# Attention's TensorE work in source order, with the products with V behind the next chunk's score tiles

## Chip, cores and metric

One core of a Trainium2 chip runs the whole program once. The time is device microseconds (us) of one execution, the median over the runs shown. The core's engines are named as in the profile: PE (TensorE: matmuls, with PEld for its weight loads), ACT (ScalarE), DVE (VectorE), POOL (GpSimd) and SP (which issues most DMAs).

## What is computed

Three stages follow each other: attention over 4 x 8 heads with queries pooled by two, a routed mixture of experts with a skip, and a gated feed-forward layer. The change touches the first stage alone.

```python
def _attn_ref(q, k, v):                      # (4, 8, 1152, 64) each
    B, H, S, D = q.shape
    factor = 2
    scale = 1.0 / np.sqrt(D)
    q_pool = q.reshape(B, H, S // factor, factor, D).mean(axis=3)
    scores = scale * np.matmul(q_pool, k.transpose(0, 1, 3, 2))
    scores = scores - np.max(scores, axis=-1, keepdims=True)
    attn = np.exp(scores)
    attn = attn / (np.sum(attn, axis=-1, keepdims=True) + 1e-09)
    return np.matmul(attn, v).astype(np.float32)

def reference(**kwargs):
    ...
    attn_out = _attn_ref(**attn_kwargs)
    B, H, S, D = attn_out.shape
    x = np.ascontiguousarray(attn_out.transpose(0, 2, 1, 3)).reshape(B * S, H * D)
    x = _moe_ref(x=x, **moe_kwargs)
    return _moe2_ref(x=x, **moe2_kwargs)
```

## The kernel before

`attention` works on two heads at a time: 16 pairs, p = 0 to 15, in a loop that begins at line 786. The 1152 keys of a head are cut into nine chunks of 128, c = 0 to 8. The 576 pooled queries of a head are cut into two halves of 288, n = 0 and 1.

For one chunk, `qk` (lines 665 to 676) makes four score tiles, one for each head h and half n. A tile is two matmuls into one PSUM tile `s`: the high parts (line 670) and the low parts with the subtracted maximum (line 671). ACT then writes the tile's exponential into the chunk's tile `P` (line 674). There are three PSUM tiles `s` (pool `ps_s`), so the fourth score tile from here waits until ACT has read this one.

`pv` (lines 689 to 695) multiplies `P` with V and adds up into the output tile `o`. Its matmuls have 64 columns: head 0 writes partitions 0 to 63 and head 1 partitions 64 to 127. A chunk has four such products, and `values` (lines 794 to 800) does two chunks at a time, c-2 and c-1, at c = 2, 4, 6 and 8; chunk 8 comes at c = 0 of the next pair. In each pair but the first, c = 4 also makes the row sums of the pair before (`sums`, line 699; `sum_up`, line 704, again with 64 columns). The sums over chunks themselves are added up on POOL (`rowsum`, line 678).

While pair p runs, the same engines prepare later pairs, as side work that `spread` sets between the steps of the loop:

- for pair p+1 the maxima of the scores: `m_tile` (line 630), 27 tiles `mx` that PE makes and DVE reduces (line 643), then `m_fin`;
- for pair p+2 the transposes of K (`t_k`, line 591, six of three blocks) and of Q (`t_q`, line 604, two of four blocks and two of one); ACT copies each out of PSUM, a K transpose with two copies, a Q transpose with three (lines 614 and 619);
- for pair p+3 the splitting of K and Q into high and low parts (`split_pieces`, line 576; on ACT lines 543 and 563), and the loads;
- in pairs 4, 5, 8, 9, 12 and 13 five blocks of the routing per batch (`Route.rows`, line 272), with a store `xd<-xr` each; in pairs 6 and 10 a ranking (`rank`).

Tiles of the side work share three PSUM tiles of the pool `ps_m`. In the last pair the weights of the first expert are loaded into buffers that attention has done with (`load_w`, line 444; group 3 into the sum buffer `acc` of pair 14, which `sums` at c = 4 reads last).

What sets the order: the steps are written down one after the other, but inside the loop a scheduler orders each engine's instructions by what it expects to be ready. So a product with V stands on PE wherever the scheduler saw a wait. Only the start-up (`ramp`, lines 522 to 774) and the later mixture of experts keep the order of the source.

Of the kernel before, what the change touches and what calls it, by code (L numbers as in the profile page):

```python
# [20 lines left out]
ET = mybir.EngineType  # L21


def spread(main, sides):
    ev = []
    for i, f in enumerate(main):
        ev.append((i, 0, len(ev), f))
    for j, (pieces, a, b) in enumerate(sides):
        pieces = list(pieces)
        for i, f in enumerate(pieces):  # L30
            ev.append((a + (b - a) * (i + 0.5) / len(pieces), 1 + j, len(ev), f))
    for e in sorted(ev, key=lambda e: e[:3]):
        e[3]()
# [3 lines left out]
def body(ctx, tc, q, k, v, w_skip, w_gate, w1, w2, m2_gate, m2_val, m2_out, out):  # L37
# [155 lines left out]
    NFG = 4  # L193
# [220 lines left out]
    def after_all(i, names):  # L414
        for a in names:
            tc.add_manual_dep(i.ins, a.name, mybir.DependencyInfo(mybir.DependencyClass.Sync, mybir.DependencyReason.DATA))
# [27 lines left out]
    def load_w(which, i, r, after=(), gs=range(NFG), pool=False):  # L444
        o, n = LIST[which]
        e = nc.values_load(info[0:1, o + i:o + i + 1], engines=(ET.Pool if pool else ET.SP,), min_val=0, max_val=E - 1)
        for g in gs:
            fs = slice(g * FG, (g + 1) * FG)
            src = w1[bass.ds(e, 1), :, fs] if r == "r1" else w2[bass.ds(e, 1), fs, :]
            d = (nc.gpsimd if pool else nc.sync).dma_start(raw[r, g][:], src.rearrange("o (c p) f -> p (o c) f", p=128))  # L450
            if not g:
                after_all(d, after)
# [18 lines left out]
    def attention(st):  # L471
# [193 lines left out]
        def qk(p, h, c, n):  # L665
            s = s_[p]
            cs = slice(c * 128, (c + 1) * 128)
            ns = slice(64 * h + n * 288, 64 * h + (n + 1) * 288)
            ps = ps_s.tile([128, 512], FP, tag="s", name="s")
            nc.tensor.matmul(ps[:, 0:288], s["ks"][:, h, cs], s["qsh"][:, h, ns], start=True, stop=False)  # L670
            nc.tensor.matmul(ps[:, 0:288], s["ks2"][0:69, h, cs], s["qsl"][0:69, h, ns], start=False, stop=True)  # L671
            if h == 0 and n == 0:
                s["P", c] = pp.tile([128, 2, 2, 288], FP, tag="P", name="P")
            i = nc.scalar.activation(s["P", c][:, h, n], ps[:, 0:288], AF.Exp, scale=0.5 / float(D) ** 0.5)  # L674
            if (h, c, n) == (0, 0, 0):
                mark[p] = i.ins.name
# [12 lines left out]
        def pv(p, c, n):  # L689
            s = s_[p]  # L690
            if c == 0 and n == 0:
                s["o"] = ps_o.tile([128, 2, 512], FP, tag="o", name="o")
            for h in range(2):
                nc.tensor.matmul(s["o"][h * 64:(h + 1) * 64, n, 0:288], s["vt"][:, h, c, :], s["P", c][:, h, n, :],  # L694
                                 start=c == 0, stop=c == NC - 1)
# [5 lines left out]
        def evac(p):  # L701
            nc.scalar.activation(xview(p), s_[p]["o"][:, :, 0:288], AF.Copy)

        def sum_up(p, src, first=True, last=True):
            if first:
                s_[p]["sm"] = ps_m.tile([128, 512], FP, tag="m", name="sm")
            for h in range(2):
                for n in range(2):
                    o = h * SQ + n * 288
                    nc.tensor.matmul(s_[p]["sm"][n * 64:(n + 1) * 64, 0:288], ones[:, 32 - 16 * h:96 - 16 * h], src[:, o:o + 288],  # L710
                                     start=first and not h, stop=last and h == 1)
# [7 lines left out]
        def sums(p):  # L719
            sum_up(p, s_[p]["acc"][:])  # L720
            sum_out(p)
            del s_[p]
# [58 lines left out]
        def sum_part(c):  # L781
            s = s_[last]
            src = s["acc"][:] if c == PEC - 1 else s["P", c][:].rearrange("p h n c -> p (h n c)")
            sum_up(last, src, c == PEC - 1, c == NC - 1)

        for p in range(NP):
            main = []
            for c in range(NC):
                pcs = [(p, c - 2), (p, c - 1)] if c and c % 2 == 0 else [] if c else [(p - 1, NC - 1)]
                for n in range(2):  # L790
                    if p or (c, n) not in early:
                        main.append(lambda c=c, n=n: qk(p, 0, c, n))

                def values(c=c, pcs=pcs):
                    if p and c == 4:
                        sums(p - 1)
                    for pc in pcs:
                        if pc[0] >= 0:
                            pv(*pc, 0)
                            pv(*pc, 1)  # L800
                main.append(values)
                main.append(lambda c=c: qk(p, 1, c, 0))
                if c == 0 and p:
                    main.append(lambda: evac(p - 1))

                def tail(c=c):
                    qk(p, 1, c, 1)
                    if p < last or c < PEC:
                        rowsum(p, c)
                main.append(tail)  # L810
            n = len(main)
            sides = []
            if not p:
                sides.append((split_pieces(2) + [lambda: load(3)], n * 0.6 / 9, n * 2 / 9))
            if p + 1 < NP:
                sides.append((m_pieces(p + 1), 0, n * 8.6 / 9))
            if p:
                sides.append(([lambda: m_fin(p, 1)], 1.5, 1.5))
            if p + 2 < NP:
                sides.append((t_pieces(p + 2, qs=False), n * 1.8 / 9, n * (5.2 if p else 6) / 9))  # L820
                sides.append((t_pieces(p + 2, ks=False), n * (5.2 if p else 6) / 9, n * (7 if p else 8) / 9))
            if p + 3 < NP:
                if p:
                    load(p + 3)
                sides.append((split_pieces(p + 3), n * (5.4 if p else 6.4) / 9, n * 8.6 / 9))
            if p + 1 < NP:
                load_v(p + 1)
            if p and p % HP == 0:
                routes.append(Route(p // HP - 1, routes[-1].scatters if routes else ()))
                bp = routes[-1].pieces()  # L830
            if p >= HP and p % HP < 2:
                rw = [lambda t=t, r=routes[-1]: r.rows(t) for t in range(G)]
                sides.append((rw[2:], 0, n * 4 / 9) if p % HP else (rw[:2], n * 5.2 / 9, n * 8.9 / 9))
            if p > HP and p % HP:
                cut = [0, *(CUT if p < last - 2 else CUL), len(bp)]
                sides.append((bp[cut[p % HP - 1]:cut[p % HP]], n * (4.5 if p == last - 2 else 1) / 9, n * (8.9 if p < last else 2.5) / 9))
            if 0 <= p - CP0 < 2 * len(first):
                if not (p - CP0) % 2:
                    cp = conv0.pieces(first[(p - CP0) // 2])
                    sides.append((cp[:1], n * 0.3 / 9, n * 0.3 / 9))  # L840
                    sides.append((cp[1:2], n * 6.5 / 9, n * 6.5 / 9))
                else:
                    sides.append((cp[2:], n * 3 / 9, n * 3 / 9))
            if p == last:
                sides.append(([list_a], n * 0.2 / 9, n * 0.2 / 9))
                sides.append(([lambda: load_w("A", 0, "r1", (), range(NFG - 1))], n * 1.5 / 9, n * 1.5 / 9))
                sides.append(([lambda: load_w("A", 0, "r1", (), range(NFG - 1, NFG))], n * 4.6 / 9, n * 4.6 / 9))
                sides.append(([lambda: load_ids("A", 0, routes[-1].scatters), lambda: gather("A", 0, 0)], n * 2.6 / 9, n * 3.5 / 9))
                pair = lambda i: psum[0]("xt")[:].rearrange("p (c n) -> p c n", c=2)
                sides.append(([lambda c2=c2: xt("A", 0, 0, c2, pair) for c2 in range(2)], n * XA / 9, n * 8.8 / 9))  # L850
                sides.append(([lambda g=g: split("r1", g, nc.gpsimd if g in AP1 else nc.vector) for g in range(3)], n * SA / 9, n * 8.8 / 9))
                sides.append(([lambda c=c: sum_part(c) for c in range(PEC - 1, NC - 1)], n * 8.3 / 9, n))
            spread(main, sides)
        sum_part(NC - 1)
        for n in range(2):
            pv(last, NC - 1, n)
# [331 lines left out]
    with ExitStack() as st:  # L1188
        routed = attention(st)
# [35 lines left out]
```

## Time and profile before

| what | value |
|---|---|
| runs | 1246.89, 1247.16, 1249.86 us; median 1247.16 us |
| profiled execution: time, span | 1245.98 us, 1244.4 us |
| PE busy, share of the span | 1183.8 us, 95% |
| PE weight loads busy | 968.2 us, 78% |
| DVE, ACT, POOL busy | 697.8, 631.3, 549.1 us |
| mean granted clock of TensorE | 0.984 of full speed |
| first score tile of pairs 0, 1, 2, 3, 7, 8, 15 | 25.9, 68.8, 100.6, 132.9, 276.7, 309.0, 554.3 us |

The span runs from the first to the last instruction. Busy time of PE is modelled: matmuls overlap, and a row's duration is longer than the distance to the next row's start, which is what one matmul costs in a stream. Of a timeline's row the first number is therefore the one to compare. A product with V is two rows of the trace for one matmul of the program; "x4" of line 694 is two products. The attention stage ends near 593 us; the stages behind it are not changed.

### The profile page before, as it was taken

What the parts mean: (1) busy time and instruction counts of PE and PEld (TensorE: products, weight loads), DVE (VectorE), ACT (ScalarE), POOL (GpSimd) and SP (SyncE); (2) the same over time, 40 slices, a digit from 0 to 9 for tenths busy, and PEclk for the clock granted to TensorE, in tenths of its full rate; (3) what the DMA queues carried; (4) which work ended last, traced back from release to release, by engine and by line L of the source; (5) the groups of instructions that cost most, each with busy time, mean ns of one, the idle gap of its engine ahead of it and who ended that gap; (6) DMA issues with size and microseconds to landing.
All of it is one profiled execution on the core that took longest, in us unless ns stands there. A gap on an engine that the chain in (4) does not pass through costs nothing. (4 is left out here: it accounts for less than half of the span.)

```text
span 1244.4 us, 19070 instructions
## 1 busy us (share of the span) xinstructions
PE 1183.8 (95%) x6950; PEld 968.2 (78%) x6950; DVE 697.8 (56%) x1379; ACT 631.3 (51%) x1440; POOL 549.1 (44%) x328
## 2 busy tenths in 40 slices
PE   5999999999999999998789987999999999999998
PEld 3777776667776777675678876788898999989997
DVE  5555565655656565664756584927447374443333
ACT  5777775777757786654245375635223141221111
POOL 5878886779857997572332353202001020100000
PEclk9899999999999999998999998999999999999999
DMA  6311122111222111003486683522102020000012
GB/s 187 84 58 58 58 75 92 41 59 58 83 68 75 59 56 46 15 19 86 130 274 203 205 283 107 167 71 68 34 18 86 1 78 24 18 1 1 10 68 76
DMA packets 76618, 99.48 MB, mean 80 GB/s; under 512 B 6600, under 2 KB 50760, under 8 KB 76490
## 3 DMA queue, kind: packets, MB, share of 16 engines
q1 hardware_dynamic: 73290, 91.05, 22.9%
q0 software_dynamic: 3200, 6.86, 1.7%
q8 instruction: 64, 1.05, 0.3%
q14 instruction: 64, 0.52, 0.2%
HBM read 84.71 MB, written 12.53 MB: 78 GB/s over the span
## 5 line engine op out<-in xcount | busy, mean ns | idle before, releaser
L643 DVE TENSOR_REDUCE m<-mx 128x1 f32<-128x384 f32 x432 | 228.8, 555 | 178.2 <-PE mx L641 175.0
L685 POOL TENSOR_TENSOR acc<-acc,P 128x1152 f32<-128x1152 f32 x106 | 281.7, 2658 | 79.5 <-ACT P L674 43.0
L1115 PE MATMUL g<-xh,wc 128*128 128x384 f32 x1152 | 303.9, 337 | 2.0 <-ACT xh L1103 2.0
L674 ACT ACTIVATE P<-s 128x288 f32<-128x288 f32 x576 | 212.4, 411 | 107.4 <-PE s L671 101.1
L1115 PEld LDWEIGHTS g<-xh,wc 128*128 128x128 f32 x1152 | 208.3, 188 | 8.8 <-ACT xh L1103 7.5
L694 PE MATMUL o<-P,vt 128*64 128x288 f32 x1152 | 207.7, 424 | 2.3 <-ACT P L674 2.3
L1115 PE MATMUL g<-xl,wc 128*128 128x384 f32 x576 | 194.5, 338 | 0.0
L670 PE MATMUL s<-qsh,ks 128*128 128x288 f32 x576 | 180.9, 322 | 2.0 <-ACT P L674 1.3
L641 PE MATMUL mx<-ks,qsh 128*128 128x384 f32 x480 | 169.5, 382 | 4.6 <-DVE lp L295 3.4
L147 POOL TENSOR_TENSOR wc<-ct,wc 128x512 fp32r<-128x512 f32 x30 | 41.7, 1402 | 290.9 <-ACT wc L146 227.9
L671 PE MATMUL s<-qsl,ks 69*128 69x288 f32 x576 | 169.7, 302 | 0.0
L1142 PE MATMUL o<-wc,ah 128*128 128x512 f32 x432 | 137.4, 395 | 3.2 <-ACT ah L1129 3.2
L670 PEld LDWEIGHTS s<-qsh,ks 128*128 128x128 f32 x576 | 110.4, 192 | 33.9 <-issue 22.3
L694 PEld LDWEIGHTS o<-P,vt 128*64 128x64 f32 x1152 | 84.3, 137 | 61.7 <-issue 22.8
L1126 DVE TENSOR_TENSOR sg<-sg,g 128x384 f32<-128x384 f32 x72 | 39.8, 552 | 147.1 <-PE g L1115 133.4
L641 PEld LDWEIGHTS mx<-ks,qsh 128*128 128x128 f32 x480 | 87.6, 193 | 44.4 <-issue 17.4
L671 PEld LDWEIGHTS s<-qsl,ks 69*128 69x128 f32 x576 | 110.5, 192 | 0.0
L1115 PEld LDWEIGHTS g<-xl,wc 128*128 128x128 f32 x576 | 108.4, 188 | 2.1 <-DVE xl L1104 0.3
L1124 ACT ACTIVATE sg<-g 128x384 f32<-128x384 f32 x72 | 35.1, 488 | 143.9 <-PE g L1115 143.9
L1142 PEld LDWEIGHTS o<-wc,ah 128*128 128x128 f32 x432 | 79.6, 188 | 20.3 <-ACT ah L1129 6.6
L1129 ACT ACTIVATE ah<-sg 128x384 fp32r<-128x384 f32 x72 | 37.6, 522 | 107.9 <-DVE sg L1126 107.9
L1142 PE MATMUL o<-wc,al 128*128 128x512 f32 x216 | 85.5, 396 | 0.6 <-DVE al L1130 0.5
(277 smaller groups left out, 1676.6 us busy)
## 6 DMA issues: line engine op xcount, KB each, us to landing
r<-in_moe_w_dram SPq DMA_DIRECT2D x28, 512.0 KB
vt<-in_v_dram SPq DMA_DIRECT2D x16, 576.0 KB
kt<-in_k_dram SPq DMA_DIRECT2D x15, 576.0 KB
qraw<-in_q_dram SPq DMA_DIRECT2D x32, 256.0 KB
xT<-in_moe_w_dram SPq DMA_DIRECT2D x14, 512.0 KB
r<-in_moe_w_gate_dram SPq DMA_DIRECT2D x12, 512.0 KB
r<-in_moe_w_val_dram SPq DMA_DIRECT2D x12, 512.0 KB
r<-in_moe_w_out_dram SPq DMA_DIRECT2D x12, 512.0 KB
```

What stands on the lines that cost most here:

```text
L147: eng.tensor_tensor(w[:, 1], t[:], w[:, 0].bitcast(FP), op=ALU.subtract)
L641: nc.tensor.matmul(ps[:, 0:384], s["qsh"][:, g, c * 128:(c + 1) * 128], s["ks"][:, g, js], start=i == 0, stop=i == len(pr) - 1)
L643: nc.vector.tensor_reduce(s["m3"][:, 5 * h + t, j:j + 1], ps[:, 0:384], axis=AX, op=ALU.max)
L670: nc.tensor.matmul(ps[:, 0:288], s["ks"][:, h, cs], s["qsh"][:, h, ns], start=True, stop=False)
L671: nc.tensor.matmul(ps[:, 0:288], s["ks2"][0:69, h, cs], s["qsl"][0:69, h, ns], start=False, stop=True)
L674: i = nc.scalar.activation(s["P", c][:, h, n], ps[:, 0:288], AF.Exp, scale=0.5 / float(D) ** 0.5)
L685: i = eng.tensor_tensor(a, s["P", 0][:] if c == 1 else a, s["P", c][:], op=ALU.add)
L694: nc.tensor.matmul(s["o"][h * 64:(h + 1) * 64, n, 0:288], s["vt"][:, h, c, :], s["P", c][:, h, n, :], start=c == 0, stop=c == NC - 1)
L1115: nc.tensor.matmul(ps[:], w[:, a, fs], b[:], start=n == 0, stop=n == 3 * KD - 1)
L1126: nc.vector.tensor_tensor(sg[:], sg[:], vv[:], op=ALU.mult)
L1129: nc.scalar.activation(ah[:], sg[:], AF.Copy)
L1142: nc.tensor.matmul(ps[:], a[:, us], w[:, b, :], start=n == 0, stop=n == 3 * GF - 1)
```

## The change

Inside the loop PE now keeps the order of the source; the other engines are still ordered by the scheduler. For c > 0 `values` is called behind the fourth score tile of its chunk, not between the heads. In the last pair the load of weight group 3 is placed at 5.1/9 of the steps, not 4.6/9, which is again behind `sums`.

```diff
--- before.py
+++ after.py
@@ -783,6 +783,8 @@
             src = s["acc"][:] if c == PEC - 1 else s["P", c][:].rearrange("p h n c -> p (h n c)")
             sum_up(last, src, c == PEC - 1, c == NC - 1)
 
+        steady = tc.manual_schedule(engines={ET.PE})
+        steady.__enter__()
         for p in range(NP):
             main = []
             for c in range(NC):
@@ -798,7 +800,8 @@
                         if pc[0] >= 0:
                             pv(*pc, 0)
                             pv(*pc, 1)
-                main.append(values)
+                if not c:
+                    main.append(values)
                 main.append(lambda c=c: qk(p, 1, c, 0))
                 if c == 0 and p:
                     main.append(lambda: evac(p - 1))
@@ -808,6 +811,8 @@
                     if p < last or c < PEC:
                         rowsum(p, c)
                 main.append(tail)
+                if c:
+                    main.append(values)
             n = len(main)
             sides = []
...
-                sides.append(([lambda: load_w("A", 0, "r1", (), range(NFG - 1, NFG))], n * 4.6 / 9, n * 4.6 / 9))
+                sides.append(([lambda: load_w("A", 0, "r1", (), range(NFG - 1, NFG))], n * 5.1 / 9, n * 5.1 / 9))
...
             spread(main, sides)
+        steady.__exit__(None, None, None)
         sum_part(NC - 1)
```

PE in pair 1, in the second half of chunk 6. In a row's names `s` is a score tile, `tq` a Q transpose, `mx` a maximum tile, `o<-P` a product with V; the numbers tell tiles apart. Before:

```order
L694 MATMUL o_928<-P_1002,vt_493 64x288 x3
L641 MATMUL mx_1103<-ks_2_112,qsh_2_118 128x384
L670 MATMUL s_1106<-qsh_1_117,ks_1_111 128x288
L671 MATMUL s_1106<-qsl_1_120,ks2_1_114 128x288
L608 MATMUL tq_1110<-idr_65,qhl_770 128x128 x4
L694 MATMUL o_928<-P_1002,vt_493 64x288
L694 MATMUL o_928<-P_1058,vt_493 64x288
L641 MATMUL mx_1118<-ks_2_112,qsh_2_118 128x384
L694 MATMUL o_928<-P_1058,vt_493 64x288 x3
L670 MATMUL s_1132<-qsh_1_117,ks_1_111 128x288
L671 MATMUL s_1132<-qsl_1_120,ks2_1_114 128x288
```

The same place with the change:

```order
L608 MATMUL tq_1112<-idr_65,qhl_776 128x128 x4
L641 MATMUL mx_1120<-ks_2_112,qsh_2_118 128x384
L670 MATMUL s_1123<-qsh_1_117,ks_1_111 128x288
L671 MATMUL s_1123<-qsl_1_120,ks2_1_114 128x288
L670 MATMUL s_1130<-qsh_1_117,ks_1_111 128x288
L671 MATMUL s_1130<-qsl_1_120,ks2_1_114 128x288
L641 MATMUL mx_1135<-ks_2_112,qsh_2_118 128x384
L608 MATMUL tq_1138<-idr_65,qhl_776 128x128
L694 MATMUL o_948<-P_1004,vt_495 64x288 x4
L694 MATMUL o_948<-P_1060,vt_495 64x288 x4
L641 MATMUL mx_1151<-ks_2_112,qsh_2_118 128x384
```

The eight products of chunks 4 and 5 stood as 3, 2 and 3 between single steps; now they stand together, behind all of chunk 6.

ACT at the same place, around the last Q transposes (`qsh`, `qsl`: copies of a transpose; `P<-s`: an exponential; `qhl`: the split of Q). Before:

```order
L674 ACTIVATE P_1101<-s_1106 128x288
L614 ACTIVATE qsh_0_116<-tq_1110 64x512 x2
L619 ACTIVATE qsl_0_119<-tq_1110 64x512
L674 ACTIVATE P_1101<-s_1132 128x288
L614 ACTIVATE qsh_0_116<-tq_1139 64x128 x2
L619 ACTIVATE qsl_0_119<-tq_1139 64x128
L674 ACTIVATE P_1101<-s_1144 128x288
L674 ACTIVATE P_1155<-s_1152 128x288
L674 ACTIVATE P_1155<-s_1157 128x288
L563 ACTIVATE qhl_1130<-qp_1129 128x10x64
```

With the change:

```order
L674 ACTIVATE P_1103<-s_1108 128x288
L614 ACTIVATE qsh_0_116<-tq_1112 64x512 x2
L619 ACTIVATE qsl_0_119<-tq_1112 64x512
L674 ACTIVATE P_1103<-s_1123 128x288
L674 ACTIVATE P_1103<-s_1130 128x288
L614 ACTIVATE qsh_0_116<-tq_1138 64x128 x2
L619 ACTIVATE qsl_0_119<-tq_1138 64x128
L563 ACTIVATE qhl_1128<-qp_1127 128x10x64
L674 ACTIVATE P_1157<-s_1154 128x288
```

ACT has the same work here; three exponentials changed sides of a copy.

## Rows read from the trace of the kernel before

**Rows 1.** The page: PE's total, and its row of DVE's reductions.
```profile
PE 1183.8 (95%) x6950; PEld 968.2 (78%) x6950; DVE 697.8 (56%) x1379; ACT 631.3 (51%) x1440; POOL 549.1 (44%) x328
...
L643 DVE TENSOR_REDUCE m<-mx 128x1 f32<-128x384 f32 x432 | 228.8, 555 | 178.2 <-PE mx L641 175.0
```

**Rows 2.** Busy time by stretch, pair 2: length, PE, PEld, DVE, ACT, POOL, clock, DMA.
```profile
100.60:132.90 32.30, 32.30 (x214) 24.36 (x213) 17.23 (x33) 24.24 (x64) 26.94 (x13) 1.00 0.18 56
```

**Rows 3.** Timeline of PE, pairs 7 and 8: start, duration, line, what, count.
```profile
303.65 0.71 PE L694 MATMUL o<-P,vt 128*64 128x288 f32 x4
...
305.71 0.34 PE L641 MATMUL mx<-ks,qsh 128*128 128x384 f32 x1
305.98 0.70 PE L694 MATMUL o<-P,vt 128*64 128x288 f32 x2
306.61 0.40 PE L670 MATMUL s<-qsh,ks 128*128 128x288 f32 x1
306.85 0.30 PE L671 MATMUL s<-qsl,ks 69*128 69x288 f32 x1
...
314.92 2.16 PE L694 MATMUL o<-P,vt 128*64 128x288 f32 x16
```

**Rows 4.** Timeline of ACT, pair 7, behind the products at c = 4.
```profile
293.75 0.86 ACT L674 ACTIVATE P<-s 128x288 f32<-128x288 f32 x2 [2.91 <-PE s L671]
294.51 0.48 ACT L598 ACTIVATE ks<-tk 128x384 fp32r<-128x384 f32 x1
...
295.25 0.70 ACT L674 ACTIVATE P<-s 128x288 f32<-128x288 f32 x2
295.83 1.20 ACT L614 ACTIVATE qsh<-tq 64x512 fp32r<-64x512 f32 x2
...
297.67 0.41 ACT L674 ACTIVATE P<-s 128x288 f32<-128x288 f32 x1
297.97 1.16 ACT L543 ACTIVATE khl<-kt 128x1152 fp32r<-128x1152 f32 x1
299.03 0.40 ACT L674 ACTIVATE P<-s 128x288 f32<-128x288 f32 x1
299.32 0.54 ACT L614 ACTIVATE qsh<-tq 64x128 fp32r<-64x128 f32 x2
...
300.17 0.71 ACT L674 ACTIVATE P<-s 128x288 f32<-128x288 f32 x2
...
305.00 0.75 ACT L563 ACTIVATE qhl<-qp 128x640 fp32r<-128x640 f32 x1
```

**Rows 5.** Timeline of PE, pair 7, the same place.
```profile
293.42 0.30 PE L671 MATMUL s<-qsl,ks 69*128 69x288 f32 x1
293.55 0.34 PE L641 MATMUL mx<-ks,qsh 128*128 128x384 f32 x1
293.73 0.29 PE L670 MATMUL s<-qsh,ks 128*128 128x288 f32 x1
...
294.00 0.38 PE L595 MATMUL tk<-idr,khl 128*128 128x128 f32 x3
294.22 0.37 PE L670 MATMUL s<-qsh,ks 128*128 128x288 f32 x1
```

**Rows 6.** Timeline of PE and of DVE, pair 5: a routing block and its store.
```profile
203.45 1.24 PE L286 MATMUL xr<-iw,xT 128*128 128x146 f32 x8
204.43 0.43 PE L641 MATMUL mx<-ks,qsh 128*128 128x384 f32 x1
...
206.92 0.56 DVE L292 TENSOR_TENSOR xr<-xr,rs 128x384 f32<-128x384 f32 x1 [1.46 <-DMA xd<-xr]
```

**Rows 7.** Busy time by stretch, and PE's timeline, in pair 0 behind the start-up.
```profile
34.00:38.00 4.00, 2.80 (x17) 1.96 (x15) 2.45 (x8) 3.89 (x9) 3.68 (x7) 0.88 0.57 102
38.00:42.00 4.00, 3.31 (x12) 2.81 (x12) 2.54 (x5) 3.40 (x9) 0.00 (x0) 0.50 0.59 169
...
39.55 0.61 PE L670 MATMUL s<-qsh,ks 128*128 128x288 f32 x1 [0.69 <-ACT qsl L619]
```

## The prediction

> **What bounds the kernel now.** I read the page first: PE is busy 95% of the span, DVE 56% [rows 1]. Then the stretches of busy time, one for each pair, cut at the first score tile. In pair 2, as in 3, 7 and 11 ("plain" pairs, without routing), PE is busy for 32.30 of 32.30 us; POOL, the next, for 26.94, ACT for 24.24 [rows 2]. So PE bounds the stage on average, and a gain has to be work that PE need not do, or does more cheaply.
>
> The Trainium skill (its page "Trainium Kernel Development and Optimization", section "Performance Expectations") calls matmul busy time a bad metric, since matmuls are pipelined, and weight-load busy time a good one. Weight loads are busy for 24.36 of the 32.30 us; by that rule up to 7.9 us of a pair might be had, by the busy row nothing.
>
> The timeline of PE shows what could be cheaper [rows 3]. Products with V cost by the slot of two, one for each head: two last 0.71 us, eight 2.16, so a slot is (2.16 - 0.71)/3 = 0.483. A lone product lasts 0.70, as long as two. So an odd burst (a row of products between other steps) pays half a slot for nothing. And each burst pays at its ends. Start to start, the burst before the score tile at 306.61 takes 0.63 us, 0.15 above its slot. The maximum tile ahead of it takes 0.27 where another takes 0.18 (293.55 to 293.73 [rows 5]): 0.09. The score matmul behind it takes 0.24 where another takes 0.13 (293.42 to 293.55 [rows 5]): 0.11. Together 0.35 us for a burst, however long.
>
> **What the change brings on PE.** In the order of PE's instructions I counted bursts of lines 694 and 710: 179 before, 80 now; 92 were odd, none is now. 99 x 0.35 = 34.7 us, and 92/2 = 46 slots x 0.483 = 22.2: together **56.9 us less work on PE**. In the last pair, 4 bursts and 5 odd ones of these (4 x 0.35 + 2.5 x 0.483 = 2.6) count for nothing: its end waits for weights whose loads come no earlier.
>
> **What it takes away.** A scattered product is also what PE does while it waits. In the second half of a pair ACT is the slower one. ACT's timeline behind the products of c = 4, pair 7 [rows 4], gives the prices, start to start: the two copies of a K transpose 0.74, of two exponentials 0.58 to 0.72, the three copies of a Q transpose of 512 columns 1.84, of 128 columns 0.85, the split of K 1.06, that of Q 0.75. ACT is hardly ever idle there, and so before the change PE filled up with products. With source order PE reaches the eight products of c = 6 too late and those of c = 8 last, and stands at a score tile until an exponential has freed `s`. ACT's order with the change, from the end of the c = 4 burst: K copies 0.74, two exponentials 0.6, Q copies 1.84, two 0.6, K split 1.06, Q copies 0.85, two 0.6, Q copies 1.84, two 0.6, Q copies 0.85, Q split 0.75: 10.3 us until only exponentials at 0.30 are left. It begins some 0.5 us in, with the first score tile, so the exponential of chunk 7's second tile ends at 11.1. That tile's buffer then takes the first score tile of chunk 8; three more at the pace of ACT and PE, and the burst of c = 8 begins near 12.9. By itself PE would be there at 9.5: 16 score tiles at 0.27 (the two starts 0.13 or 0.14 [rows 5]) are 4.3, a K transpose 0.22 ([rows 5]: 294.00 to 294.22), ten blocks of Q at a third of that 0.7, ten maxima at 0.18 and a small transpose 2.0, together 7.2; the burst of c = 6 adds 2.3 (four slots and 0.35). So **3.4 us are lost in each of the 14 pairs that prepare Q for p+2: 47.6**. Before, from 293.2 to 309.0, this stretch took 15.8 us with eight products more; the working gives 12.9 + 2.3 = 15.2 after, so a plain pair gains little there. Bounds for the loss: 2.5 if ACT starts with tiles left over and copies less late, 4.3 if the first exponential comes 0.9 later; I take the middle, since the durations are rows of the same place. That is +-12.6 over 14 pairs.
>
> Some work hides in this wait. In pairs 4, 8 and 12 two routing blocks are PE's there, eight matmuls of which take 203.45 to 204.43, 0.98 [rows 6]; I take 1.75 of the two. For the 12 narrow matmuls of a ranking in pairs 6 and 10 I take 0.6, between 0 and 12 at the 0.13 of a score matmul, 1.6. 3 x 1.75 + 2 x 0.6 = **6.4 back**. For small waits elsewhere (a maximum tile that DVE is late with, where a product no longer steps in) I allow 0.2 in 13 pairs: **2.6**; bounds 0, and 0.85 each (a rival below).
>
> **Edits that cost nothing.** V's later place issues no DMA and no work for another engine. The `P` tiles are read a chunk's step later; POOL and ACT had spare time for that [rows 2]. On POOL the split and sum of Q move one row sum ahead; POOL has 32.30 - 26.94 = 5.4 us a pair idle. On SP the load of V stands one place later, and in pairs 5 and 9 the first routing store is behind three more loads of Q. That makes what waits for the store late, which is DVE (below), and behind it PE's tile; the loads behind it come a pair ahead of their use. The weight group at 5.1/9 comes (0.5/9) x 34 = 1.9 us later and is used after attention, which then still has some 15 us to run: nothing, and 1.9 at most if that cover is gone.
>
> **Sum.** -56.9 + 2.6 + 47.6 - 6.4 + 2.6 = -10.5. Against the profiled execution's own 1245.98 that is 1235.5; the median of the runs is 1.2 above it, so **1237 us**.
>
> **Rivals.**
>
> *The clock falls (slower).* In pair 0, where ACT copies transposes and PE waits for it, the granted clock went from 0.88 to 0.50 of full speed, 1.2 GHz, with PE busy for 2.80 of 4 us and a wait of 0.69 [rows 7]. The change makes such a stretch in 14 pairs, PE waiting for ACT a third of the time. Then the burst of c = 6 takes 4.6 for 2.3, and the ACT-bound wait can't hide it: 14 x 2.3 = 32, 1269 us; in half of the pairs 1253. From 5 pairs on it uses up the gain. Against it: the score tiles between waits go on, and PE has some 70% of the stretch's time in work, more than in that row.
> The Trainium skill ("TensorE: Matmul & The Clock Gate", "Why this matters for your kernels") asks only for no long idle gaps between bursts; by that rule waits of some tenths of a microsecond leave the clock alone, and this rival has no chance. The trace differs: the clock is at 0.50 around a wait of only 0.69 [rows 7]. Chance 0.22.
>
> *Three tiles in `ps_m` (same).* DVE takes 0.555 for a maximum [rows 1]; ten of them lie between the bursts of c = 2 and c = 4: 5.55 against PE's own 4.7 there (eight score tiles 2.2, ten maxima 1.8, three K transposes 0.7). If PE waits for DVE in order, 0.85 x 13 = 11 is lost: 1248. For it: DVE's idle time ahead of these ended nearly always with PE [rows 1], so now DVE is ahead; against, three buffers smooth that. Chance 0.16.
>
> *The routing's stores are hidden (faster).* In pair 5, DVE waits 1.46 us for the store `xd<-xr` [rows 6], twice a pair in six pairs: 17.5 us. If it lies beside the new wait for ACT, it no longer counts: 1219. Against: in pairs 5, 9 and 13 the blocks stand ahead of c = 4, outside that stretch. Chance 0.10.
>
> *The change doesn't bring what it says.* If the 0.35 is not the price of a switch but a wait for the score tile or for P, a burst fewer brings nothing, and only 22.2 of slots is gained: about 1270. Against: the same excess stands at bursts of every length. Chance 0.05.
>
> **How the numbers follow.** 0.47 is left for my forecast of 1237, whose own bounds give 1224 to 1250. The range, 1217 to 1266, adds the same-case, most of the routing's stores and most of the clock's; it leaves out the dearest part of the clock (0.07), the price rival (0.05) and tails of the first (0.06). A measurement tells 0.3%, 3.7 us, from no change: faster is 0.40 of my forecast's, 0.10 of the stores' and 0.05 of the others'; same 0.05 of mine, 0.10 of the maxima's and 0.03 of the clock's; slower 0.19 of the clock's, the price's 0.05 and tails of 0.03.
>
> **What would show it.** Right: 80 bursts, mostly of 2.1 us start to start; plain pairs of 31 to 33 us; PE waits some 45 us in all for ACT's `P` ahead of line 670, between chunks 5 and 8 of pairs 0 to 13; granted clock at 1.00 there; pairs 4 to 6 shorter by two microseconds or more than before. Wrong: the wait at line 670 below 25 or above 65 us; a clock below 0.95 in the pairs; idle time of PE that DVE's `m` ends; bursts whose neighbours still take 0.27 and 0.24.

## The result and the profile after

The change takes 1261.51 us (median of 4 runs, 1259.25 to 1264.03) against 1247.3 before: 1.0121 of before, interval 1.0098 to 1.0145. It is slower, by 14 us where the forecast had 10 less. (Each ratio in this text is against the kernel before as measured beside that run, with medians of 1247.3 to 1250.4, so equal times can have unequal ratios.)

The page of the profile after (for the rows of before, [rows 1]):

```profile
PE 1166.0 (93%) x6950; PEld 977.5 (78%) x6950; DVE 696.0 (55%) x1379; ACT 630.9 (50%) x1440; POOL 550.3 (44%) x328
...
L643 DVE TENSOR_REDUCE m<-mx 128x1 f32<-128x384 f32 x432 | 230.4, 555 | 204.6 <-PE mx L641 197.8
...
L670 PE MATMUL s<-qsh,ks 128*128 128x288 f32 x576 | 181.6, 321 | 16.1 <-ACT P L674 14.2
```

PE is busy for 17.8 us less than before, and the span is 13.2 us longer (1257.6 against 1244.4). So PE does cost less, and stands still more.

Where in the program? The stretches of busy time are cut here at the small transpose of maxima half a chunk into each pair (line 654), in both traces alike; the first number is the length, the last but two the granted clock. Before, all of pairs 1 to 13, then pairs 2, 3, 4 and 15:

```profile
68.12:526.26 458.14, 454.72 (x2926) 330.22 (x2925) 271.15 (x618) 326.86 (x846) 357.29 (x166) 1.00 0.19 60
101.27:133.56 32.29, 32.29 (x214) 24.35 (x213) 17.23 (x34) 24.23 (x64) 26.93 (x13) 1.00 0.18 56
133.56:165.81 32.25, 32.25 (x214) 24.26 (x213) 19.00 (x39) 25.09 (x66) 26.86 (x13) 1.00 0.19 56
165.81:201.49 35.68, 35.68 (x235) 26.13 (x233) 21.62 (x51) 25.39 (x66) 28.67 (x13) 1.00 0.23 73
...
554.96:592.00 37.04, 33.71 (x199) 20.83 (x198) 18.52 (x30) 17.13 (x42) 13.96 (x9) 0.91 0.26 72
```

After, all of pairs 1 to 13, then pairs 1, 2, 3, 4 and 15:

```profile
73.16:545.75 472.59, 439.64 (x2920) 335.98 (x2919) 273.67 (x618) 325.35 (x843) 354.51 (x164) 0.95 0.19 58
73.16:106.24 33.08, 30.99 (x215) 23.58 (x213) 17.37 (x34) 24.25 (x64) 24.26 (x12) 1.00 0.18 55
106.24:140.17 33.93, 32.09 (x214) 24.38 (x213) 17.27 (x34) 24.31 (x64) 27.84 (x13) 0.95 0.19 55
140.17:176.26 36.09, 33.61 (x214) 24.95 (x213) 19.31 (x39) 25.16 (x66) 29.12 (x14) 0.91 0.22 64
176.26:210.85 34.59, 32.89 (x234) 26.02 (x233) 21.89 (x51) 25.03 (x66) 25.61 (x12) 1.00 0.20 65
...
572.88:607.80 34.92, 29.85 (x199) 20.14 (x198) 17.55 (x30) 17.07 (x42) 11.50 (x9) 0.90 0.27 77
```

Attention ends 15.8 us later (607.8 against 592.0): pair 0 takes 5.0 more (to 73.16 against 68.12), pairs 1 to 13 take 14.5 more (472.59 - 458.14), pairs 14 and 15 together 3.7 less. (The cut puts some 1.3 us on pair 0 that pairs 1 to 13 lose: before, pair 1's transpose stands at 68.12, ahead of the pair's first score tile at 68.8, while in pair 2 it stands behind it, at 101.27 against 100.6. So pair 1 after is compared with pair 2 before, which does the same work.) Behind attention 2.6 come back; why was not followed up. The clock tells the pairs apart. Pair 4, with two routing blocks behind c = 4 and a clock of 1.00, is 1.1 faster than before. Pair 3, at 0.91, is 3.8 slower.

One place makes it. Pair 2 in steps of 2 us, from the end of the c = 4 burst to the c = 6 burst:

```profile
124.00:126.00 2.00, 1.68 (x14) 1.43 (x13) 1.11 (x2) 1.99 (x5) 0.00 (x0) 1.00 0.00 0
126.00:128.00 2.00, 1.66 (x11) 1.18 (x10) 1.37 (x2) 1.97 (x4) 0.52 (x1) 1.00 0.00 0
128.00:130.00 2.00, 0.85 (x4) 0.63 (x4) 0.56 (x1) 1.95 (x7) 2.00 (x1) 0.87 0.00 0
130.00:132.00 2.00, 2.00 (x10) 1.19 (x11) 0.56 (x1) 1.95 (x5) 2.00 (x3) 0.50 0.00 0
132.00:134.00 2.00, 2.00 (x15) 0.87 (x11) 0.00 (x0) 1.59 (x5) 2.00 (x2) 0.77 0.12 6
```

ACT (fourth busy number) is full. PE (the first) falls to 0.85 of 2 us, and the granted clock drops to 0.50, 1.2 GHz, behind it. The timeline of PE shows what it stood for (in brackets: the wait ahead of a row). Pair 2, and behind it the same place in pair 1:

```profile
125.68 0.33 PE L654 MATMUL mt<-idr,m 128*128 128x128 f32 x1 [0.32 <-DVE m L643]
...
126.66 0.45 PE L641 MATMUL mx<-ks,qsh 128*128 128x384 f32 x1 [0.34 <-ACT qsl L619]
...
128.16 0.29 PE L671 MATMUL s<-qsl,ks 69*128 69x288 f32 x1
129.60 0.61 PE L670 MATMUL s<-qsh,ks 128*128 128x288 f32 x1 [1.15 <-ACT P L674]
...
130.80 3.18 PE L694 MATMUL o<-P,vt 128*64 128x288 f32 x16
133.91 0.45 PE L641 MATMUL mx<-ks,qsh 128*128 128x384 f32 x1
```

```profile
92.61 0.33 PE L654 MATMUL mt<-idr,m 128*128 128x128 f32 x1 [0.32 <-DVE m L643]
...
93.59 0.44 PE L641 MATMUL mx<-ks,qsh 128*128 128x384 f32 x1 [0.34 <-ACT qsl L619]
...
96.54 0.40 PE L670 MATMUL s<-qsh,ks 128*128 128x288 f32 x1 [1.16 <-ACT P L674]
...
97.24 2.16 PE L694 MATMUL o<-P,vt 128*64 128x288 f32 x16
99.33 0.44 PE L641 MATMUL mx<-ks,qsh 128*128 128x384 f32 x1
```

Three short waits, the longest 1.15 us. Then the burst of c = 6 takes 3.11 from start to start. Pair 1 has the same three waits and keeps the clock at 1.00, and there the same burst takes 2.09 (97.24 to 99.33). So these waits can bring the clock down and don't always; what decides between the two is not shown. The five largest kinds of wait of PE from 70 to 550 us (total, times, longest; five smaller kinds add 5.5 us):

```profile
PE s L670 <- ACT P L674: 8.0, 7, 1.2
PE mx L641 <- ACT qsl L619: 7.1, 13, 1.0
PE tq L608 <- DVE m L643: 5.1, 8, 0.9
PE mt L654 <- DVE m L643: 3.8, 12, 0.3
PE mx L641 <- DVE lp L295: 2.6, 3, 0.9
```

Before, the whole list was one row, 3.4 us. Now waiting is spread over all that PE shares with others: `s`, but more the three tiles of `ps_m`, which ACT's copies and DVE's maxima give back.

### The profile page after: what moved, and what is told of

Same layout as the page of the kernel before. It is cut to its first block, busy times and chain, and to the rows that moved or that the text cites. A ratio compares the mean times of both kernels' runs of the same rounds, so it can differ in the third digit from the quotient of the medians.

```text
span 1257.6 us, 19059 instructions
## 1 busy us (share of the span) xinstructions
PE 1166.0 (93%) x6950; PEld 977.5 (78%) x6950; DVE 696.0 (55%) x1379; ACT 630.9 (50%) x1440; POOL 550.3 (44%) x328
## 5 line engine op out<-in xcount | busy, mean ns | idle before, releaser
L641 PE MATMUL mx<-ks,qsh 128*128 128x384 f32 x480 | 176.8, 389 | 13.0 <-ACT qsl L619 7.1
L694 PE MATMUL o<-P,vt 128*64 128x288 f32 x1152 | 171.2, 440 | 0.0
L641 PEld LDWEIGHTS mx<-ks,qsh 128*128 128x128 f32 x480 | 92.2, 199 | 43.8 <-issue 18.4
```

Of the source, the lines that this page charges most:

```text
L641: nc.tensor.matmul(ps[:, 0:384], s["qsh"][:, g, c * 128:(c + 1) * 128], s["ks"][:, g, js], start=i == 0, stop=i == len(pr) - 1)
```

## Experiments

Two theories stood. By the **clock theory** the loss is the lower clock behind PE's waits for ACT. By the **waiting theory** it is what PE loses in order, at whatever clock.

**The two parts alone.** First source order, with the products between the heads as before:

```diff
-                if not c:
-                    main.append(values)
+                main.append(values)
...
-                if c:
-                    main.append(values)
```

> Source order on PE alone; the products with V stay between the heads, where they were written before. 81 bursts, all even, as in the change (80). Clock theory (what costs is that PE, waiting for ACT around the last Q transposes, gets the lower clock): here the products of c = 6 come two score tiles earlier, inside that wait, and those of c = 4 come before the second half of chunk 4, so PE has less left to wait with behind them; the clock falls in fewer pairs (under 30 us at the lower clock between pairs 1 and 13, against 47.6), and the time lies at 1240 to 1255. Waiting theory (PE loses what it waits for ACT in order, at whatever clock, and the place of the burst only moves it): 1258 to 1266, the same as the change. A third way, that the products now wait for exponentials of the chunk before: above 1266, with PE waits at the product's line.

Measured: 1261.51 us, 1.0077 of before (1.0052 to 1.0101). Plain pairs behave as the clock theory wants, and routing pairs do not. Pairs 3 and 5, and the two longest kinds of waits:

```profile
139.38:172.05 32.67, 31.31 (x214) 23.57 (x213) 19.28 (x39) 24.86 (x66) 27.29 (x13) 1.00 0.19 55
...
208.33:253.67 45.34, 39.95 (x245) 30.00 (x243) 23.30 (x57) 25.48 (x66) 25.93 (x13) 0.89 0.19 60
```

```profile
PE mx L641 <- ACT qsl L619: 9.0, 15, 1.0
PE mx L641 <- DVE lp L295: 6.6, 5, 2.1
```

Pair 3 keeps the full clock and takes 32.67, 0.4 more than before. Pair 5 takes 45.3 against 40.5: a maximum tile stands behind a routing block (`lp`) that waits for its store, up to 2.1 us, and the clock falls there too. So the time lies in the waiting theory's range, but for neither theory's reason: one place mended, another broken.

The move of the products alone, in the scheduler's order:

```diff
-        steady = tc.manual_schedule(engines={ET.PE})
-        steady.__enter__()
...
-        steady.__exit__(None, None, None)
```

> The other part of the change alone: the products with V are written behind the four score tiles, but the scheduler orders PE as before. 189 bursts, 94 odd, against 179 and 92 before. Clock theory and waiting theory alike: PE has scattered products to fill its waits with, no new stretch at the lower clock in pairs 1 to 13, and ten bursts more at 0.35 us cost 3.5: 1247 to 1254. If the place behind four tiles itself did the harm (products too late for the buffers of P), the time would come near the change, 1258 or more.

Measured: 1240.23 us, 0.9922 (0.9900 to 0.9943): faster than before, which was not expected. Pairs 1 to 13, and pair 15:

```profile
70.47:524.51 454.04, 452.91 (x2921) 332.13 (x2919) 272.49 (x618) 324.99 (x843) 357.56 (x166) 1.00 0.20 60
...
553.12:585.00 31.88, 30.85 (x197) 19.40 (x198) 17.41 (x29) 17.03 (x42) 11.83 (x8) 1.00 0.30 84
```

Pairs 1 to 13 are 4.1 us shorter, all of it in the pairs with routing or a ranking; plain pairs 2, 3, 7 and 11 are 0.4 to 0.9 longer. Pair 15 is 5.2 shorter, at a clock of 1.00 where before it had 0.91. Why the products' new place keeps the clock there was not separated. It isn't the later weight load: with that edit alone the instructions of every engine stand in the order of before. So the slower part of the change is the source order.

**Work into the wait.** The products of c = 6 cut in two, the four of chunk 4 between the heads of chunk 6:

```diff
-                    for pc in pcs:
+                    for pc in (pcs[1:] if c == 6 else pcs):
...
+                elif c == 6:
+                    main.append(lambda: [pv(p, 4, n) for n in range(2)])
```

> The change, with the eight products of c = 6 cut in two: the four of chunk 4 between the heads of chunk 6, where PE waits for ACT, the four of chunk 5 behind it. 16 bursts more, 16 x 0.35 = 5.6 us more work on PE. Clock theory: the clock stays up in most pairs (under 20 us at the lower clock in pairs 1 to 13), which gives back up to half of the difference to 47.6, some 14 to 20 us, and some of the waits are filled: 1238 to 1252. Waiting theory: the wait moves behind the burst, and the time is the change's plus up to 5.6, 1260 to 1268.

Measured: 1256.13 us, 1.0043 (1.0018 to 1.0069). Pairs 1 to 13 and pair 3, and PE in pair 2:

```profile
73.80:535.90 462.10, 431.06 (x2920) 326.15 (x2919) 272.30 (x618) 321.73 (x843) 354.48 (x164) 0.99 0.20 59
...
138.46:171.49 33.03, 31.46 (x214) 23.54 (x213) 19.02 (x39) 24.68 (x66) 27.60 (x14) 1.00 0.19 55
```

```profile
126.73 0.44 PE L641 MATMUL mx<-ks,qsh 128*128 128x384 f32 x1
127.10 1.19 PE L694 MATMUL o<-P,vt 128*64 128x288 f32 x8
128.22 0.54 PE L608 MATMUL tq<-idr,qhl 128*128 128x128 f32 x4
```

Where PE stood before it now streams products; the clock stays, and pairs 1 to 13 are 10.5 us shorter than with the change although PE does 13 x 0.35 = 4.6 more. Time without PE work is nearly the same (462.10 - 431.06 = 31.0 us against 472.59 - 439.64 = 33.0); it is the busy time that shrinks. That is the clock theory's sign. The total falls between the two expected ranges: with the clock back, plain pairs still take 32.3 to 33.0 and not less than before.

**More work that brings nothing.** Each block of a Q transpose made three times:

```diff
-            for i in range(n):
+            for i in [j for j in range(n) for _ in range(3 if p > 1 else 1)]:
```

> The change, with each block of a Q transpose in pairs 0 to 13 transposed three times into the same place: 20 blocks more a pair, at 0.07 to 0.085 us each 1.5 us, together some 21 us of PE work that computes nothing new, right in the stretch where PE waits for ACT. Clock theory: the stretch keeps the full clock more often, so at least some of the 47.6 us at the lower clock go away, and the time falls or stays although PE does more: 1246 to 1261. Waiting theory: the extra work hides in the waits at best, and the time is 1261 to 1275.

Measured: 1274.21 us, 1.0190 (1.0157 to 1.0223). Pairs 1 to 13, then pairs 9 and 13:

```profile
72.92:550.39 477.47, 455.02 (x3180) 359.67 (x3179) 273.03 (x618) 326.76 (x843) 357.28 (x165) 0.96 0.19 57
...
363.11:402.90 39.79, 36.75 (x264) 29.17 (x263) 23.09 (x57) 25.65 (x66) 26.77 (x13) 1.00 0.21 66
...
510.01:550.39 40.38, 36.75 (x264) 29.20 (x263) 25.05 (x66) 24.50 (x65) 21.08 (x9) 1.00 0.10 32
```

By the total this is the waiting theory's range. But pairs 1 to 13 are only 4.9 us longer than with the change, for 13 x 1.5 = 19.5 us of extra work: time without PE work falls from 33.0 to 22.5, and pairs 9 and 13 now keep the full clock, at 0.9 us less each than with the change. Some 7 us of the total lie in the stages behind attention (657 us against 650), which the edit does not touch. So most of the empty work is paid for by the waits and the clock, and the total alone would mislead.

**A shorter wait.** The third copy of a Q transpose on DVE:

```diff
-                nc.scalar.activation(s["qsl"][0:64, h, c], psf[64:128, 0:n * 128], AF.Copy)
+                if p > 1:
+                    nc.vector.tensor_copy(s["qsl"][0:64, h, c], psf[64:128, 0:n * 128])
+                else:
+                    nc.scalar.activation(s["qsl"][0:64, h, c], psf[64:128, 0:n * 128], AF.Copy)
```

> The change, with the third copy of each Q transpose (the low part, 0.59 us for 512 columns and 0.28 for 128 in the trace of the change) on DVE in pairs 0 to 13 and not on ACT: 1.75 us a pair off ACT, and a Q transpose leaves its PSUM tile that much earlier. If the wait for ACT at the Q transposes is the cause, of the lost time and of the lower clock behind it: the 2.7 us that plain pairs wait fall to some 1.2, the lower clock leaves most of pairs 1 to 13 (44 us to under 15), plain pairs 2, 3, 7 and 11 last 30.5 to 31.5 us, and the time is 1225 to 1243. If the loss lies elsewhere (source order between all engines, DVE's maxima being late): DVE gets later by 1.75 us a pair, plain pairs stay at 33 us or more, time 1252 to 1268.

Measured: 1259.28 us, 1.0074 (1.0052 to 1.0096). As a whole it lies in the range of a loss elsewhere, and the clock theory's expectation is missed; but it gives the best price of the clock. Pairs 1, 2 and 3:

```profile
70.64:103.74 33.10, 32.11 (x215) 24.43 (x213) 19.23 (x38) 22.65 (x60) 27.16 (x13) 0.95 0.19 55
103.74:135.35 31.61, 30.58 (x214) 23.65 (x213) 19.23 (x38) 22.64 (x60) 25.63 (x12) 1.00 0.20 57
135.35:170.81 35.46, 33.66 (x214) 24.84 (x213) 21.09 (x43) 23.74 (x62) 30.89 (x15) 0.90 0.23 67
```

Pairs 1 and 2 are the same work with the same two waits (0.3 for DVE's maximum, 0.5 for the copy on DVE), and 0.99 and 1.03 us without PE work (33.10 - 32.11, 31.61 - 30.58). In one the clock fell and in the other it did not, and that is 1.5 us. In the change's own trace pairs 1 and 2 differ by 0.85 for 1.00 against 0.95. Pair 3 has a conversion on DVE more, which now also holds back the Q transposes: PE waits 0.6 us more there, in front of one of them.

Both together, the split and the copy on DVE:

> The split of the products of c = 6 and the low copy on DVE together, in source order. If both act on the same wait: clock up in nearly all of pairs 1 to 13, plain pairs at 30 to 31.5 us (17.3 regular work, 10.5 of slots, 3 for the ends of six bursts and small excess), 1222 to 1242. If the low copy only moves the wait to DVE: plain pairs at 32.3 to 33 as with the split alone, 1250 to 1258.

Measured: 1244.84 us, 0.9984 (0.9956 to 1.0011), with a clock of 1.00 over pairs 1 to 13 and plain pairs of 31.3 (1 and 2) and 32.8 (3): between the two expectations, no different from before.

The same copy on DVE in the scheduler's order, with the products moved:

> The scheduler's order on PE, the products with V behind the four tiles (which alone gave 0.992 of before), and the low copy on DVE. In this order PE has products to fill its waits with, so ACT's relief is worth little: plain pairs 32 to 33 us, time 1232 to 1243. If ACT's relief helps in any order: below 1230. If DVE is then the late one: above 1243.

Measured: 1243.12 us, 0.9959 (0.9939 to 0.9980), at the upper edge of what was expected: where PE fills its waits anyway, ACT's relief brings nothing over the move alone (0.9922).

**The last pair.** Source order ends before pair 15:

```diff
         for p in range(NP):
+            if p == 1:
+                steady.__enter__()
+            if p == last:
+                steady.__exit__(None, None, None)
```

> The change, with source order on PE ending before pair 15; only pair 15's order differs from the change's (products scattered as in the scheduler's order). In the change PE stands 5.0 us in pair 15 for an exponential that is queued on ACT behind the splitting of a weight whose load is not there, and the clock falls behind it. If that stand is the price of source order there: pair 15 goes from 34.9 to 31 to 33 us as in the moved products alone (31.9), time 2 to 4 us under the change's, 1257 to 1260. If it is not: as the change, 1261, or above.

Measured: 1260.29 us, 1.0094 (1.0059 to 1.0129). Pair 15 itself took 32.1 us against 34.9, as expected. The total's interval holds the change's, so it shows no more. (The edit also begins the source order at pair 1, but in the trace PE's order in pair 0 is the change's; pair 0 ordered by the scheduler was not tried.)

**All the waits.** With the split, the copy on DVE and pair 15 to the scheduler, three edits of side work:

```diff
-            r.insert(20, lambda: m_fin(p, 0))
+            r.insert(24 if p else 20, lambda: m_fin(p, 0))
...
-                sides.append((rw[2:], 0, n * 4 / 9) ...
+                sides.append((rw[2:], 0, n * 6 / 9) ...
...
-                    sides.append((cp[1:2], n * 6.5 / 9, n * 6.5 / 9))
+                    sides.append((cp[1:2], n * 8 / 9, n * 8 / 9))
```

> Source order with the split products of c = 6 and the low copies on DVE (together 0.998 of before), and four waits that its trace still shows taken away: pair 15 left to the scheduler (35.7 to 32 us), the small transpose of maxima four tiles later in the list (0.74 us a pair in 14 pairs), the conversion on DVE at 8/9 of a pair and not at 6.5/9 (1.0 us in pairs 3, 7 and 11), and the routing blocks of pairs 5, 9 and 13 spread over 6/9 of the pair and not 4/9 (up to 4 us a pair of waits for the store and for DVE). If these waits are PE's own loss in source order: 3.7 + 10 + 3 + 6 to 12 less, 1218 to 1230, 0.975 to 0.985 of before. If each wait only moves to the next place where PE stands: 1238 to 1248.

Measured: 1235.72 us, 0.9883 (0.9865 to 0.9900), between the two expectations. In this kernel and the next three the last routing block of pair 5 or 9 reads sums that the next pair's have overwritten, so the experts get other rows; their times stand for attention alone.

> The scheduler's order with the products behind four tiles (0.992 of before), and the same three edits of the side work (transpose of maxima, conversion, routing blocks later). Here PE fills waits with products, so the edits should be worth nothing in plain pairs and at most the 2 to 4 us that the routing pairs lose: 1234 to 1242, 0.988 to 0.994. If waits of DVE and of the store cost time in this order too: below 1232.

Measured: 1239.12 us, 0.9923 (0.9898 to 0.9948), the same as the move alone, as expected.

> As the source order with the sides moved, but the routing blocks of pair 13 stay at 4/9 of the pair, since the choice of experts of pair 13 reads them from 4.5/9 on; those of pairs 5 and 9 stay at 6/9. Attention ended at 578 us in the former's trace against 592 before the change and 608 with the change; pair 13 may lose its 0 to 2 us again. With the stages behind attention as long as before the change (652 us): 1229 to 1238, 0.983 to 0.990 of before. If the lower clock comes back in pairs 5, 9 and 13: 1238 to 1243.

Measured: 1233.03 us, 0.9857 (0.9832 to 0.9882), as expected.

> As the scheduler's order with the sides moved, with the same mending in pair 13. Its trace showed plain pairs at 33.5 us (32.7 to 33.2 without the edits) and the routing pairs at 37.1 (38.3 to 39.5): the edits of plain pairs cost a little, those of routing pairs bring 1 to 2 us each: 1236 to 1243, 0.989 to 0.994, no different from the moved products alone.

Measured: 1241.71 us, 0.9930 (0.9907 to 0.9952), as expected. In these runs, taking away waits of DVE and of the store was worth something only where PE stands in order behind them.

**The same with the blocks early enough** (e14), at 4.4/9, which keeps the row sums whole; then once more with the burst of c = 6 whole:

> Source order in pairs 0 to 14 with the products of c = 6 split, low copies of Q transposes on DVE, the transpose of maxima four tiles later, the conversion at 8/9 of a pair, and the routing blocks of pairs 5 and 9 spread to 4.4/9 of the pair (no further, since the next pair's row sums overwrite what they read). Its forerunner with the blocks at 6/9 showed plain pairs of 31.2 to 31.6 us and 101 bursts; pairs 5 and 9 may be 1 to 3 us longer here. 1231 to 1240, 0.985 to 0.992 of before. Waits that only move: above 1243.

Measured: 1232.36 us, 0.9864 (0.9837 to 0.9890), as expected, and faster than both kernels, before and with the change.

> The same with the eight products of c = 6 in one burst behind chunk 6, as in the change: 16 bursts fewer than in e14, 5.6 us less work on PE. Clock theory: the stretch at the Q transposes has less for PE to do and the lower clock comes back in most of pairs 2 to 13 (over 30 us against under 17 in e14); the time is 8 to 18 us above e14's, 1240 to 1256. If the clock costs little by itself, or the waits were all that mattered: 3 to 6 us below e14's.

Measured: 1235.18 us, 0.9881 (0.9860 to 0.9903): the same as the split within the intervals, and not what either theory said, because the clock did not come down. Pairs 1 to 13, then 3 and 6 of the whole burst:

```profile
69.90:516.23 446.33, 422.19 (x2921) 328.00 (x2919) 297.12 (x670) 305.48 (x791) 358.26 (x165) 1.00 0.21 61
...
132.79:164.44 31.65, 30.69 (x214) 23.69 (x213) 21.03 (x43) 23.57 (x62) 27.34 (x13) 1.00 0.20 57
...
236.42:271.21 34.79, 31.85 (x220) 23.97 (x219) 23.80 (x60) 23.96 (x63) 28.72 (x14) 1.00 0.24 68
```

Against the copy on DVE alone (pair 3: 35.46 at 0.90) this differs in plain pairs by the maxima's transpose and the conversion, two waits of DVE. With these gone the clock stays at 1.00 in every plain pair, split or not. PE does the change's matmuls here in the change's bursts, and is busy for 422.2 us in pairs 1 to 13 against 439.6 with the change: about 17 us of busy time go with the clock. And in the trace of the split, pairs 4 and 8, the same work on PE:

```profile
164.57:199.37 34.80, 33.36 (x234) 25.88 (x233) 23.64 (x55) 23.27 (x62) 29.20 (x14) 1.00 0.26 79
...
302.47:338.48 36.01, 34.73 (x234) 27.14 (x233) 23.65 (x55) 23.26 (x62) 31.58 (x16) 0.95 0.27 75
```

Again 1.2 us for a clock of 0.95.

## Why the prediction was wrong

**Fewer bursts: right.** 80 bursts, none odd. The steps around a burst still take 0.10 more than elsewhere, with no wait in the rows (133.91 to 134.19 for a maximum tile behind a burst, 0.28 against 0.18). The prediction listed just that among its signs of being wrong, but the sign was ill chosen: a price for each burst, however long, stays on the bursts that are left. What tells is the sum: in a plain pair, where 10 bursts, 4 of them odd, become 5, the forecast is 5 x 0.35 + 2 x 0.483 = 2.7 us. There the products take 12.23 us start to start before (pair 3) and 10.46 in the whole-burst kernel, 1.8 less; with five ends of 0.20 on the neighbours some 2.8. The rival that the 0.35 is a wait falls.

**The waits: right in place and sum, wrong in kind.** I had 3.4 us a pair at line 670, 45 in all, and 2.6 in all for small waits elsewhere. Line 670 has 8.0, and the other kinds in PE's list add up to 24.1. The chain of ACT that I added up to 10.3 us is there (123.46 to some 133.6 in pair 2, [rows 4] by step), but I followed it to `s` alone. A Q transpose also holds one of three `ps_m` tiles for its 1.8 us of copies, and the maximum behind it waits (0.34 at 126.66). In a plain pair at full clock the terms together came out: 3.4 + 0.2 - 2.7 = 0.9 us longer by the forecast, and pair 1 takes 33.08 against 32.29 for the same work before, 0.8 longer. That the waits add up to the forecast although their places differ is partly luck. The rival of three tiles in `ps_m` held in part: PE waits for DVE's maxima (`m`) 11.4 us in all, near the 11 it named, but mostly in other places than between c = 2 and c = 4.

**The clock: the step that failed.** The sum has nothing for the clock: it takes every pair at 1.00. I gave the rival 0.22, because PE has "some 70% of the stretch's time in work, more than in that row". It had more on average (1.68 and 1.66 of 2 us), yet not at the end, where the waits come together (0.85 of 2). The rival's mechanism and place were right; the clock fell in 9 of the 13 pairs, all but 1, 4, 8 and 12, and in pair 0. Its price was too high where it put it: 2.3 us more for the burst of c = 6, where pair 2 shows 1.0 (3.11 against 2.09). That its 1253 for half of the pairs and 1269 for all stand on both sides of the measured 1261.5 is therefore partly luck. Its price from rows: against 1.00 the clocks of these 13 pairs lack 0.58 in sum, 11.6 times 0.05; at 0.85 to 1.5 us for each 0.05 that is 10 to 17 us, of the 14.5 (15.8 without the effect of the cut) that pairs 1 to 13 lost. Pair 0 had the same stand at its end: 66.78 to 68.32, then a burst of 3.2 us, and lost 5.0 (3.7 without the effect of the cut), where I expected a gain.

I also misread the row that I weighed it by. Its wait of 0.69 us stands behind the fall: the granted clock is 0.51 from 37.0 to 38.0 us, and the wait ends at 39.55 [rows 7]. Ahead of the fall, before the change, stand two others:

```profile
35.17 0.53 PE L608 MATMUL tq<-idr,qhl 128*128 128x128 f32 x4 [0.80 <-ACT P L674]
...
36.24 0.62 PE L641 MATMUL mx<-ks,qsh 128*128 128x384 f32 x2 [0.41 <-ACT qsh L614]
```

What I wrote against the rival from the Trainium skill ("TensorE: Matmul & The Clock Gate", "Why this matters for your kernels"), that the page asks only for no long idle gaps between bursts and short waits so leave the clock alone, is not what the change's trace shows: the clock fell in these pairs, and no wait of PE between 70 and 550 us was longer than 1.2.

**Smaller steps.** The routing blocks did hide in pairs 4, 8 and 12: 1.0 to 1.1 us less each than before, where the forecast's terms make it 1.7 (11 bursts, 6 of them odd, become 5: 3.55 less, 1.75 hidden, 3.6 of waits). The clock stayed at 1.00 there; that the blocks held it up was not tried. In pairs 5, 9 and 13 they did not: PE waits for DVE behind a block, 2.6 us in all, and the clock falls. The rival that the stores' waits vanish brought no time: pair 5 is no shorter. That the last pair gains nothing was nearly right: 2.1 less, but with a new stand of 5.0 us for an exponential, queued on ACT behind a weight's split. In the scheduler's order this pair took 32.

**Shown and not shown.** Shown: the source order makes the loss and the move does not (the two parts alone); work in the wait brings most of the clock back (the split), and less waiting the rest (split with the copy on DVE, and the whole burst with the waits mended), though the copy alone did not; and a clock of 0.95 over a pair of the same work costs 0.85 to 1.5 us. Only estimated: how the 14.5 us of pairs 1 to 13 divide between clock and waits, for only pair 1 has the change's waits at the full clock. Open: why the same waits bring the clock down in one pair and not in the other.

## What to carry to other kernels

A scattered cheap operation can be the filler that hides an engine's waits: before grouping it, add up what each shared buffer will then wait for, not one chain alone, and take the clock into the sum, since on PE several waits close together can cost more than their length. If the order is written by hand, mend the waits first: with a copy on the idler engine and side work moved off the waiting stretch, source order went from 1.012 to 0.988 of before with the same bursts, the last pair left to the scheduler. Compare stretch by stretch too: a total also holds the drift of stages that no edit touched. And try the parts of a change one by one; here one part was 0.8% faster and the other 0.8% slower.

## What the runs showed of the hardware

The granted clock fell to 1.2 GHz behind three waits of 0.32, 0.34 and 1.15 us within 4.3, with PE at work in between. It is a close thing: in the same trace pair 1 kept 1.00 with waits of 0.32, 0.34 and 1.16, and with the copy on DVE pair 2 kept 1.00 and pair 1 had 0.95 with equal waits. Where it falls, the burst behind is the one to pay, 3.1 us instead of 2.1.
